# One planner for another on VectorE's side work in an attention and token-mixing block

## The chip, the cores and the metric

One core of a Trainium2 chip runs the whole program. The metric is the device time of one execution in microseconds (us). Each kernel is timed in several executions and the median is given; beside the times there is one execution recorded by the hardware profiler, whose trace has every instruction on TensorE (matrix products; PE in the profile, PEld for its weight loads), VectorE (DVE), ScalarE (ACT), GpSimd (POOL) and SyncE (SP, which issues the DMAs).

## The reference

The block has two halves with residual connections, each modulated by six vectors that come from a condition c. Sizes: S = 2048 rows, D = 512, H = 32 heads of 16, F = 1792.

```python
mod = (silu(c) @ w_mod).reshape(c.shape[0], 6, 1, -1)   # sa, ca, ga, sb, cb, gb
h = layernorm(x) * (1 + ca) + sa
x = x + ga * A(h)          # A: attention over a sliding window of 256 keys, then @ wo
h = layernorm(x) * (1 + cb) + sb
x = x + gb * B(h)          # B: layernorm(h), then an MLP over the rows (tokens):
                           # u = gelu(einsum('bsd,sf->bdf', h, w1) + b1)
                           # y = einsum('bdf,fs->bds', u, w2) + b2, transposed back
```

So every row block passes three layer norms: the first before the projections, the second after attention, and the third, the last, at the start of B.

## The kernel before

The rows are sixteen blocks of 128 (`xres[0..15]`), in four stages `tg` of four blocks. The program has a set-up (to 15.6 us: condition vector, first norm of stage 0, its first Q, K and V), an attention part, and then the MLP.

**Attention, units and sets.** Attention runs as 80 units `(tg, g8, k)`: stage, group of eight heads, and one of five kinds `k`. In texts, units are numbered u = 20 tg + 5 g8 + k, and ul = 5 g8 + k is the place in the stage. Five units with one `(tg, g8)` are called a set. Kinds k = 0, 2 (even heads) and k = 3, 4 (odd heads) compute whole 128-row tiles of scores, and k = 1 the remaining half tiles of both. A unit does, in the program's order:

1. two exponentials on ScalarE (L535), each over a PSUM tile `pss` of 1024 columns (for k = 0 and 3 of stage 0, 512), with other work between them;
2. the scores of the next unit on TensorE (L486 and L513, with masks added by L494 and L522), which read `QT` and `KT` of their set;
3. where k = 1 or 4, the end of a half of the heads: the last products with V (L566) into `po`, and on VectorE the transpose of `po` to `t2` (L592), which frees `po`;
4. a group of dense products (L250) into the one PSUM tile `dn`, for instance Q, K or V for some heads of this stage or the next, the output projection of a finished row block (`wo_group`), or TensorE transposes of normed rows (L232); and an instruction that empties `dn` ("the emptying"), mostly on VectorE: `QT` L291, `ks` L294, `VaugT` L270, `x` L347, `h1T` L240, `part` L676;
5. the products of the previous unit's exponentials with V (L546, L566).

Each engine works in the program's order. `dn` and `po` are single buffers, so the next group waits for the emptying, and the next half of the heads for the transpose. `pss` has three buffers.

**VectorE's side work** is cut into steps which are placed among the units as the program is built:

- quotient: reciprocal of the softmax sums (`zr`, L600), then on GpSimd the product with them (`merge`, L601); then `back`, the transpose back into `OTd` (L608), which `wo_group` reads in the next stage;
- first norm: statistics (`ln1_stats`, L211, L212), on GpSimd a power for 1/sigma (L198, L202), the application (`xn1`, L218), read by TensorE's transposes of the next stage;
- second and third norm (`ln23`, for row blocks 0 to 11): statistics of `x` (p1), application into `h2` (L623) with two products on GpSimd (L634, L635) (p2), statistics of `h2` (p3), application into `hb` (L623) (p4). `hb` is read by four early groups of the MLP (`part_group`, units 72 to 79) and by the MLP.

In the kernel before, each step has a cost in us and a gap in units to the next step of its chain. `run_dve` (L650) is called once per unit, behind the second exponential and ahead of the emptying, with a budget of what `now` is ahead of `load`; `now` grows by 1.5 or 1.9 per unit, and `load` by the costs that were placed. It takes steps chain after chain while they fit.

**Groups** are laid at fixed places of each stage in `plan` (L683). K of stage 0's first two head groups is masked into even and odd heads on VectorE, all others on GpSimd (`KT`, L297).

**Loads.** SP issues all DMAs in the program's order. `at_unit` (L723) puts four w_mod loads at units 1 to 4, `wod` at unit 6, and from unit 22 on one row block of w1 (448 KB) per unit into `w1a`, which takes the place of the released `wmod`. The rest of w1 and w2 are loaded behind the attention part.

**The MLP** (L828, L915, L935) follows, with the last four row blocks' output projection and norms (L847 to L891) among the first.

Of the kernel before, what the change touches and what calls it, by code (L numbers as in the profile page):

```python
# [12 lines left out]
P = 128  # L13
# [11 lines left out]
NA = 11  # L25


@with_exitstack
def kernel(
# [28 lines left out]
    small = ctx.enter_context(tc.tile_pool(name="small", bufs=4))  # L58
# [111 lines left out]
    npool = tc.alloc_tile_pool(name="npool", bufs=2)  # L170
    NG = NT // 4
# [44 lines left out]
    def ln1_apply(tg, tl):  # L216
        xn1[tg, tl] = xp.tile([P, D], DT.bfloat16, name="xn1")
        nc.vector.tensor_scalar(  # L218
            out=xn1[tg, tl][:], in0=xres[4 * tg + tl][:], scalar1=ln1[tg][:, tl, 0:1],
            scalar2=ln1[tg, tl // 2][:, tl % 2 : tl % 2 + 1], op0=ALU.subtract, op1=ALU.mult,  # L220
        )
# [147 lines left out]
    with tc.manual_schedule():  # L369
# [223 lines left out]

        def norm_rest(tg, g8):
# [3 lines left out]
            def quotient():  # L598
# [5 lines left out]
                )  # L604

# [3 lines left out]
            return [(quotient, 0.4, 1), (back, 0.7, 0)]  # L609


        def ln23(tb):
# [9 lines left out]
            def apply(out, src, key):  # L622
                nc.vector.tensor_scalar(  # L623
# [4 lines left out]
            def p1():  # L628
                stats(xres[tb][:], "m2")

            def p2():
                v["h2"] = npool.tile([P, D], DT.bfloat16, name="h2")
                apply(v["h2"][:], xres[tb][:], "m2")
                nc.gpsimd.tensor_tensor(out=v["h2"][:], in0=v["h2"][:], in1=bc_cb1[:], op=ALU.mult)  # L634
                nc.gpsimd.tensor_tensor(out=v["h2"][:], in0=v["h2"][:], in1=bc_sb[:], op=ALU.add)  # L635

            def p3():
                stats(v["h2"][:], "m3")

            def p4():  # L640
                done.add(tb)
                apply(hb[tb][:], v["h2"][:], "m3")
            return [(p1, 0.9, 2), (p2, 0.45, 2), (p3, 0.9, 2), (p4, 0.45, 0)]

        dve = []

        def add_dve(u, ps):
            dve.append([list(ps), u])

        def run_dve(u, budget):  # L650
            spent = 0.0
            for chain in dve:
                while chain[0] and chain[1] <= u and spent + chain[0][0][1] <= budget:
                    f, cost, gap = chain[0].pop(0)
                    f()
                    spent += cost
                    chain[1] = u + gap
            dve[:] = [c for c in dve if c[0]]
            return spent
# [20 lines left out]
        BC = ((4, bc_cb1, True), (2, bc_ga, False), (5, bc_gb, False), (3, bc_sb, False))  # L680
        wo_next = iter(range(12))

        def plan(tg):  # L683
# [6 lines left out]
            for n in range(2, 4):  # L690
                lay(n - 2, v_group(tg, n, ps_dn, act=tg == 0))
            own = ((2, 1, "q"), (3, 1, "k"), (4, 2, "k"), (5, 2, "q"), (6, 3, "k"), (7, 3, "q")) if tg == 0 else (
                (3, 1, "q"), (4, 2, "k"), (5, 2, "q"), (6, 3, "k"), (8, 3, "q"))
            for ul, g8, kind in own:
                lay(ul, qk_group(tg, g8, kind, ps_dn))
            if tg == 0:
                lay(8, bias_group(ps_dn))
                for ul, (v, dst, add1) in zip((9, 17, 18, 19), BC):
                    lay(ul, bc_group(v, dst, add1, ps_dn))
                then[17] = [(lambda g=g: fold_wod(g), 0.45, 0) for g in range(ND)]  # L700
            for ul in {0: (), 1: (7, 9, 10, 14), 2: (7, 9, 10, 14), 3: (7, 9, 10, 11)}[tg]:
                tb = next(wo_next)
                lay(ul, wo_group(tb, ps_dn))
                then[ul] = ln23(tb)
            if tg + 1 < NG:
                t0, t1, k0, v0, q0, k1, v1 = (10, 11, 12, 13, 14, 15, 16) if tg == 0 else (11, 12, 13, 15, 16, 17, 18)
# [4 lines left out]
                for ul, g8, kind in ((k0, 0, "k"), (q0, 0, "q"), (k1, 1, "k")):  # L711
                    lay(ul, qk_group(tg + 1, g8, kind, ps_dn))
# [267 lines left out]
```

## Time and profile before

| | us |
|---|---|
| median of 3 timed runs (lowest to highest) | 294.87 (294.27 to 297.1) |
| the profiled execution, its own time | 295.69 |
| its span, first to last instruction | 294.0 |
| busy: TensorE / VectorE / ScalarE / GpSimd | 256.3 / 170.5 / 170.2 / 99.2 |
| first exponential starts, last ends | 15.59, 193.51 |
| in 18.00 to 195.70: TensorE / VectorE / ScalarE / GpSimd busy | 148.09 / 123.88 / 146.59 / 84.52 |
| MLP: first product, last output product | 195.71, 290.0 |

The span is that of one recorded execution; its own time is 1.7 us longer than its span. Busy times say little by themselves: in the attention part no engine is busy all the time, and what sets the length is read from what each engine waits for. A row of the profile names line, engine, operation and tiles; "idle before ... <-" is the time in which the engine had nothing to run, and the instruction that ended that wait. "issue" there means that the engine waited for nothing that the profile shows. TensorE's granted clock was 0.99 on the mean; from 4.77 us on it was 1.0, but for 0.5 from 32.08 to 35.49 us.

### The profile page before, as it was taken

How to read it: one execution, taken by the hardware profiler on the slowest of the kernel's cores; microseconds unless marked ns; L12 is line 12 of the kernel's file. 1: busy time of each engine (PE TensorE's matmuls, PEld its weight loads, DVE VectorE, ACT ScalarE, POOL GpSimd, SP SyncE). 2: the span in 40 equal slices, each digit the busy share in tenths (PEclk: the TensorE clock that was granted, in tenths of full speed). 3: DMA queues.
4: the chain of work that ended last, by engine and by line, in shares of the span. 5: the costliest groups of instructions: out<-in, count | busy, mean ns of one | idle time of the engine just before them, and what ended most of it. 6: DMA issues, size and time to landing. Idle time of an engine off the chain costs nothing.

```text
span 294.0 us, 12957 instructions
## 1 busy us (share of the span) xinstructions
PE 256.3 (87%) x5960; PEld 140.6 (48%) x5960; DVE 170.5 (58%) x358; ACT 170.2 (58%) x192; POOL 99.2 (34%) x163
## 2 busy tenths in 40 slices
PE   6867798995696987888986998989999999999994
PEld 2534355553454654555654655644444444444441
DVE  6465477665387778687777667888911100505253
ACT  7567677897587899789898898933008220000000
POOL 5020343311134784375486656594410000000000
PEclk9999799999999999999999999999999999999999
DMA  6958000059200000000000000089950000112031
GB/s 195 345 174 291 4 4 6 4 193 401 102 6 2 4 4 4 6 3 4 4 4 4 4 4 4 4 274 401 419 224 1 2 0 0 36 39 71 0 107 36
DMA packets 15386, 24.95 MB, mean 85 GB/s; under 512 B 2276, under 2 KB 11492, under 8 KB 15332
## 3 DMA queue, kind: packets, MB, share of 16 engines
q1 hardware_dynamic: 15332, 24.13, 22.9%
q8 instruction: 46, 0.75, 1.1%
q14 instruction: 8, 0.07, 0.1%
HBM read 22.03 MB, written 2.10 MB: 82 GB/s over the span
## 4 chain that ended last, share of the span: by engine, by line
PE 68%; DVE 16%; POOL 5%; issue 4%; DMA 2%; ACT 2%; SPq 1%; DVEq 0%
PE dn L250 17%; PE py L935 16%; PE pu L828 7%; PE pu L915 7%; PE pss L513 4%; PE po L566 4%; PE pss L486 4%; DVE t L592 4%; PE po L546 3%; POOL merge L601 3%; DMA wmod<-in_w_mod_dram 2%; ACT et L535 2%; DVE zr L600 2%; DVE ks L294 2%; PE pss L494 1%
## 5 line engine op out<-in xcount | busy, mean ns | idle before, releaser
L535 ACT ACTIVATE et<-pss 128x1024 bf16<-128x1024 f32 (+1 forms) x160 | 146.7, 980 | 28.8 <-PE pss L494 20.0
L935 PE MATMUL py<-guT,w2r 128*128 128x512 bf16 x224 | 48.5, 380 | 0.0
L942 DVE SCALAR_TENSOR_TENSOR o<-py,bFM,bc_gb 128x512 bf16<-128x512 f32 x16 | 11.4, 747 | 45.1 <-PE py L935 45.1
L250 PE MATMUL dn<-h1T,wqkv 128*32 128x512 bf16 x512 | 34.3, 390 | 3.6 <-DVE h1T L240 1.5
L486 PE MATMUL pss<-QT,KT 32*128 32x192 bf16 (+2 forms) x704 | 26.3, 240 | 10.1 <-DVE QT L291 3.7
L935 PEld LDWEIGHTS <-w2r 128*128 128x128 bf16 x224 | 21.9, 98 | 26.4
L601 POOL TENSOR_TENSOR merge<-t,zr 128x512 bf16<-128x512 f32 x16 | 17.0, 1060 | 40.7 <-DVE zr L600 40.7
L592 DVE STREAM_TRANSPOSE t<-po 128x512 f32<-128x512 f32 x32 | 22.9, 716 | 12.8 <-PE po L566 12.2
L546 PE MATMUL po<-et,VaugT 128*32 128x192 bf16 (+2 forms) x704 | 25.6, 242 | 3.7 <-DVE t L592 2.1
L546 PEld LDWEIGHTS <-VaugT 128*32 128x32 bf16 x704 | 17.2, 97 | 17.7 <-issue 5.8
L202 POOL TENSOR_TENSOR ln_rstd<-ln_ve,mhalf 128x1 f32<-128x1 f32 (+1 forms) x40 | 24.0, 599 | 3.3
L198 POOL TENSOR_SCALAR ln_ve<-ln_mv 128x1 f32<-128x1 f32 (+1 forms) x40 | 9.7, 243 | 43.3 <-DVE ln_mv L212 20.5
L486 PEld LDWEIGHTS <-KT 32*128 32x128 bf16 x704 | 11.7, 93 | 20.7 <-issue 14.6
L566 PE MATMUL po<-et,VaugT 64*32 64x64 bf16 x960 | 19.2, 193 | 2.0 <-DVE VaugT L270 1.4
L494 PE MATMUL pss<-mask_q,mask_k 32*128 32x64 bf16 (+1 forms) x736 | 18.7, 197 | 1.8 <-issue 1.8
L291 DVE CAST QT<-dn 128x512 bf16<-128x512 f32 x15 | 10.3, 687 | 15.0 <-PE dn L250 11.0
L250 PEld LDWEIGHTS <-wqkv 128*32 128x32 bf16 x512 | 11.8, 97 | 13.9 <-issue 3.8
L250 PE MATMUL dn<-wqkv,h1T 128*32 128x512 bf16 x256 | 16.6, 381 | 0.7 <-DVE ks L294 0.5
L297 POOL TENSOR_SCALAR KT<-ks,mask_even 128x512 bf16<-128x512 bf16 x14 | 9.7, 691 | 21.8 <-DVE ks L294 21.8
L494 PEld LDWEIGHTS <-mask_k 32*128 32x128 bf16 x736 | 15.7, 94 | 2.3 <-issue 2.1
L566 PEld LDWEIGHTS <-VaugT 64*32 64x32 bf16 x960 | 11.1, 92 | 11.4 <-issue 5.6
L513 PE MATMUL pss<-QT,KT 32*64 32x64 bf16 x1024 | 14.6, 195 | 1.6 <-issue 1.5
(112 smaller groups left out, 358.2 us busy)
## 6 DMA issues: line engine op xcount, KB each, us to landing
w2r<-in_B_w_dram SPq DMA_DIRECT2D x14, 512.0 KB, 9.9
w1a<-in_B_w_dram SPq DMA_DIRECT2D x11, 448.0 KB, 8.2
wmod<-in_w_mod_dram SPq DMA_DIRECT2D x6, 512.0 KB, 5.7
w1b<-in_B_w_dram SPq DMA_DIRECT2D x5, 448.0 KB, 6.1
x<-in_A_x_dram SPq DMA_DIRECT2D x16, 128.0 KB, 3.3
out_dram<-otile SPq DMA_DIRECT2D x16, 128.0 KB, 1.7
wqkv<-in_A_wqkv_dram SPq DMA_DIRECT2D x2, 384.0 KB, 5.7
wqkv<-in_A_wqkv_dram SPq DMA_DIRECT2D x1, 512.0 KB, 6.5
```

What stands on the lines that cost most here:

```text
L202: nc.gpsimd.tensor_tensor(out=r[:], in0=ve[:], in1=mhalf[:, 0:n], op=ALU.pow)
L250: nc.tensor.matmul(out[cols, :], lhsT=lhsT[:, cols], rhs=rhs, start=start, stop=stop, tile_position=(0, 32 * j), skip_group_check=True,)
L486: nc.tensor.matmul(pss[j // 2][:, j % 2, c0 : c0 + nq], lhsT=keys(kb, g8, par)[rows[j], k0 : k0 + P], rhs=QT[tg][g8][rows[j], q0 : q0 + nq ...
L494: nc.tensor.matmul(pss[j // 2][:, j % 2, c0 : c0 + 64 * nb].rearrange("p (b q) -> p b q", q=64), lhsT=mask_k[rows[j], P * what : P * what ...
L513: nc.tensor.matmul(pss[a][64 * half : 64 * half + 64, j % 2, c0 : c0 + 64], lhsT=keys(kb, g8, par)[rows[j], k0 : k0 + 64], rhs=QT[tg][g8][ ...
L535: act = nc.scalar.activation(out=et[:, :, 0:n], in_=state.pop((u, a))[:, :, 0:n], func=ACT.Exp, scale=SCORE_SCALE,)
L546: nc.tensor.matmul(state["po"][32 * j : 32 * j + 32, q0 : q0 + nq], lhsT=VaugT[kb // 4][:, kb % 4, 8 * g8 + 2 * j + par, :], rhs=state["e" ...
L566: mm = nc.tensor.matmul(state["po"][32 * j : 32 * j + 32, q0 : q0 + 64], lhsT=VaugT[kb // 4][part64, kb % 4, 8 * g8 + 2 * j + par, :], rhs ...
L592: nc.vector.transpose(out=state["t2"][:, par, :], in_=state["po"][:])
L601: nc.gpsimd.tensor_tensor(out=m[:].rearrange("p (b a d) -> p a b d", a=2, d=DH), in0=t2v[:, :, :, 0:DH], in1=zr[:].to_broadcast([P, 2, 16, ...
L828: nc.tensor.matmul(pu[:, i, :], lhsT=w1_of(sc, fc), rhs=hb[sc][:], start=(sc == 0), stop=(sc == NT - 1),)
L935: nc.tensor.matmul(pys[tl][:], lhsT=w2r[:, fc, tb * P : (tb + 1) * P], rhs=guT[fc][:], start=(fc == 0), stop=(fc == NF - 1),)
```

## The change

The lists of VectorE's steps are now placed with a running estimate of each engine's time (`clock`), kept as the program is built: TensorE, ScalarE, VectorE, GpSimd, and the times at which `dn` and `po` come free. `fill(until)` places steps whose estimated start and end lie ahead of `until`; a step whose predecessor's GpSimd work has not come back by the estimate waits. It is called before `po` is transposed, before each emptying, and at the end of a unit.

The first norm's application goes from VectorE to GpSimd for stages 1 to 3, and that of the third norm (`hb`) for row blocks 0 to 11, now issued together with its statistics. `h2` has a pool of four buffers of its own, and at most four blocks are between p2 and p3. Statistics of stages 2 and 3 are computed in stage 0. Q, K, V, `wo` and `bc` groups are laid at other units; the unit without a group changes from ul 2 and 19 (stage 1, 2), 2 (stage 3) to ul 16 and 19 (stage 1, 2), 11 (stage 3). Each w1 row block is loaded in two halves of 224 KB by 22 DMAs. The number of matmuls is the same.

```diff
-    small = ctx.enter_context(tc.tile_pool(name="small", bufs=4))
+    small = ctx.enter_context(tc.tile_pool(name="small", bufs=6))
...
+    lnpool = tc.alloc_tile_pool(name="lnpool", bufs=LIVE)
...
     def ln1_apply(tg, tl):
         xn1[tg, tl] = xp.tile([P, D], DT.bfloat16, name="xn1")
-        nc.vector.tensor_scalar(
+        (nc.gpsimd if tg else nc.vector).tensor_scalar(
...
-            return [(quotient, 0.4, 1), (back, 0.7, 0)]
+            return [(quotient, 0.36), (back, 0.72)]
...
             def p3():
                 stats(v["h2"][:], "m3")
-
-            def p4():
+                apply(nc.gpsimd, hb[tb][:], v["h2"][:], "m3")
                 done.add(tb)
-                apply(hb[tb][:], v["h2"][:], "m3")
-            return [(p1, 0.9, 2), (p2, 0.45, 2), (p3, 0.9, 2), (p4, 0.45, 0)]
+                live.discard(tb)
+                return 1.54
+            return [(p1, 0.88), (p2, 0.37, lambda: len(live) < LIVE), (p3, 0.88)]
...
-        def run_dve(u, budget):
-            spent = 0.0
-            for chain in dve:
-                while chain[0] and chain[1] <= u and spent + chain[0][0][1] <= budget:
...
+        def on_pool(cost):
+            clock["pool"] = max(clock["pool"], clock["dve"]) + cost
+            return clock["pool"] + 0.1
+
+        def fill(until):
+
+            while True:
+                for chain in chains:
+                    f, cost, *free = chain[0][0]
+                    start = max(clock["dve"], chain[1])
+                    if start + cost <= until and start < clock["dve"] + 0.3 and all(x() for x in free):
+                        break
+                else:
+                    break
+                chain[0].pop(0)
+                clock["dve"] = start + cost
+                given = f()
+                chain[1] = on_pool(given) if given else clock["dve"]
+                chains[:] = [c for c in chains if c[0]]
...
             if tg == 0:
+                for ul, g8, kind in ((2, 1, "k"), (3, 1, "q"), (4, 2, "k"), (5, 2, "q"), (6, 3, "k"), (7, 3, "q")):
+                    qk(ul, tg, g8, kind)
                 lay(8, bias_group(ps_dn))
-                for ul, (v, dst, add1) in zip((9, 17, 18, 19), BC):
+                for ul, (v, dst, add1) in zip((9, 16, 17, 18), BC):
...
+            else:
+                for ul, g8, kind in ((2, 1, "q"), (3, 2, "k"), (4, 2, "q"), (5, 3, "k"), (8, 3, "q")):
+                    qk(ul, tg, g8, kind)
+                for ul in (6, 7, 9, 10):
...
-                t0, t1, k0, v0, q0, k1, v1 = (10, 11, 12, 13, 14, 15, 16) if tg == 0 else (11, 12, 13, 15, 16, 17, 18)
+                t0, t1, k0, v0, q0, k1, v1 = (10, 11, 12, 13, 14, 15, 19) if tg == 0 else (11, 12, 13, 14, 15, 17, 18)
...
-                w1box["sc"] = iter(range(NA))
-
-            sc = next(w1box.get("sc", iter(())), None)
-            if sc is not None:
-                dma.dma_start(out=w1box["a"][:, sc, :], in_=w1box["v"][:, sc, :])
+                w1box["sc"] = iter([(sc, n) for sc in range(NA) for n in range(2)])
+
+            for sc, n in [x for x in [next(w1box.get("sc", iter(())), None)] if x]:
+                part_f = slice(n * F // 2, (n + 1) * F // 2)
+                dma.dma_start(out=w1box["a"][:, sc, part_f], in_=w1box["v"][:, sc, part_f])
...
             if closes:
+                clock["pe"] += 0.23
+                fill(clock["pe"])
                 close_head_set(*closes, behind)
-                load += 0.75
+                clock["dve"] = max(clock["dve"], clock["pe"] + 0.05) + 0.73
...
             emit_exp(u, 1)
-            load = max(load, now - 0.5)
-            now += 1.5 if (tg, k) in ((0, 0), (0, 3)) else 1.9
-            load += run_dve(u, min(now - load, 1.3 if group and group[2] else 1.9))
+            clock["act"] = max(clock["act"], ready[u][1]) + half
             if group:
-                group[1](tile_)
-                load += group[2]
+                fill(clock["pe"] + 0.05)
+                evacuate(group, tile_, tg == 0 and ul < 2)
...
+            fill(clock["pe"])
             at_unit(tg, ul, u)
```

## The prediction

> **What bounds the kernel now.** I read the busy times by stretches of 25 us first, then the start of every exponential on ScalarE (two per unit, so 80 unit lengths), then the waits inside the attention stage, then the order of time around its longest gaps. From 195.7 us on TensorE never pauses, as in this stretch (columns: length, then busy us of PE, PEld, DVE, ACT, POOL, then clock and DMA):
>
> ```profile
> 225.00:250.00 25.00, 25.00 (x118) 11.33 (x116) 1.99 (x4) 5.54 (x9) 0.00 (x0) 1.00 0.00 1
> ```
>
> So the last 98 us are TensorE's, and the change leaves their matmuls alone. The attention stage (15.6 to 193.5) is where time is lost. A set of five units repeats sixteen times; four sets, by the same view:
>
> ```profile
> 84.93:96.67 11.74, 9.27 (x360) 6.13 (x345) 8.84 (x18) 9.70 (x12) 4.18 (x8) 1.00 0.02 4
> 150.76:162.49 11.73, 8.07 (x344) 5.29 (x329) 8.64 (x17) 9.67 (x12) 8.18 (x12) 1.00 0.02 4
> 162.49:172.77 10.28, 9.79 (x376) 6.09 (x362) 7.93 (x15) 9.57 (x11) 6.08 (x12) 1.00 0.02 5
> 183.54:193.51 9.97, 9.10 (x336) 5.49 (x336) 8.16 (x18) 9.56 (x11) 6.69 (x10) 1.00 0.13 42
> ```
>
> ScalarE works 9.6 us in every set and TensorE 8.1 to 9.8; the sets last 9.97 to 11.7. The floor is 9.97: ScalarE is then idle 0.4 us. The twelve sets from 59.64 to 193.51 take 133.87 us, 14.2 over twelve floors. What TensorE waits for there (total us, times, longest):
>
> ```profile
> PE pss L486 <- DVE QT L291: 3.7, 3, 1.6
> PE po L546 <- DVE t L592: 2.1, 3, 1.0
> PE dn L250 <- DVE ks L294: 2.1, 4, 0.9
> PE dn L232 <- DVE h1T L240: 1.8, 2, 1.2
> PE dn L250 <- DVE x L347: 1.6, 2, 0.9
> PE po L566 <- DVE VaugT L270: 1.4, 2, 1.2
> PE pss L494 <- issue: 1.8, 2, 1.4
> ```
>
> VectorE is not full (7 to 9 us a set): its few urgent steps, which empty PSUM, stand behind others. The order of time shows one case, a long norm pair ahead of V, then a wait for GpSimd ahead of Q, each with TensorE's stall:
>
> ```profile
> 156.59 1.38 DVE L623 TENSOR_SCALAR h<-x,ln_mv,ln_rstd 128x512 bf16<-128x512 bf16 x2
> 157.89 0.68 DVE L270 CAST VaugT<-dn 128x512 bf16<-128x512 f32 x1
> ...
> 160.25 0.69 DVE L617 BATCH_NORM_STATS2 ln_stats<-h 128x6 f32<-128x512 bf16 x1 [1.06 <-POOL h L635]
> 161.07 0.66 DVE L291 CAST QT<-dn 128x512 bf16<-128x512 f32 x1
> ```
>
> ```profile
> 158.62 0.21 PE L566 MATMUL po<-et,VaugT 64*32 64x64 bf16 x4 [1.23 <-DVE VaugT L270]
> 161.88 0.40 PE L486 MATMUL pss<-QT,KT 32*128 32x256 bf16 x12 [1.40 <-DVE QT L291]
> ```
>
> A second cause: three stalls that no engine ended, at 67.06 (1.44 us), 73.14 (1.47) and 77.97 (1.79), 4.70 together. The trace's packets of the instruction queue, 16 KB each, begin at 64.72, 70.78 and 75.59: TensorE resumes 2.34 to 2.38 us after each. They fall in or just behind the eleven w1 loads (62 to 75.5 us, about 380 GB/s: 5.05 MB in 13.3 us):
>
> ```profile
> 67.06 0.20 PE L494 MATMUL pss<-mask_q,mask_k 32*128 32x64 bf16 x2 [1.44 <-issue]
> 73.14 0.40 PE L546 MATMUL po<-et,VaugT 128*32 128x256 bf16 x10 [1.47 <-issue]
> 77.97 0.39 PE L486 MATMUL pss<-QT,KT 32*128 32x64 bf16 x10 [1.79 <-issue]
> ```
>
> So 14.2 us over the floor are 4.7 of code loading and 9.5 of late VectorE.
>
> **The change, part by part.** The sum is against the profiled execution, span 294.0, time 295.69, which is 0.82 above the median of the three runs; I apply the difference to the median.
>
> *VectorE's order.* In the built program of the changed kernel, from unit 21 on, a unit mostly issues on VectorE one step that empties PSUM for a group and one other: with k = 1 the transpose of po, k = 2 the reciprocal (L600), k = 3 the transpose back (L608), k = 4 the transpose of po; statistics, now often two together, stand in k = 0, the longest unit (2.24 us), and only in unit 79 does a norm step stand ahead of the transpose of po in its unit. Two steps of 0.69 to 0.72 us, with 0.35 for the reciprocal, are below the 1.82 to 2.19 us of such a unit. In k = 0 two statistics at 0.85 (0.67 + 0.18) and an emptying at 0.69 make 2.39 against 2.24, but the transpose that normally follows comes after the next group's matmuls, so I cost it at nothing; its cover gone, it is 0.15 us each in some ten units. Where does the stall go? ScalarE is next. I take 10.2 us a set, between the best set (9.97) and the best set that follows a late one (10.28), instead of (133.87 - 4.70) / 12 = 10.76: 12 x 0.56 = -6.8. Bounds: 10.45, the mean of sets 130.06 to 150.76 and 162.49 to 183.54, gives -3.8; the floor gives -9.5.
>
> *Moved to GpSimd.* Twelve first norms (L218; the first four blocks stay) and twelve last norms (hb, L623) leave VectorE. Beside GpSimd's work the moved kind is slow: xn1 applies in the stage take 0.40 us with GpSimd idle and 0.67 with it busy, the longest 1.31. So VectorE loses 12 x 0.47 to 0.56 plus 12 x 0.42, about 11 of 124 us; that is part of the term above. GpSimd gains 24 instructions. No first norm is on GpSimd in the trace; the nearest row is the K masking, same shape and kind:
>
> ```profile
> L297 POOL TENSOR_SCALAR KT<-ks,mask_even 128x512 bf16<-128x512 bf16 x14 | 9.7, 691 | 21.8 <-DVE ks L294 21.8
> ```
>
> I take 0.69, with 1.16 (L634) as the upper bound: 16.6 to 27.8 us more on 84.5 of 178. GpSimd's queue is then busy 61 to 67% of a stage of 167 us, and these results are due 3 to 10 units later, so I cost them at nothing, +4 if a late answer reaches TensorE in a third of the sets (1.03 us each, the row L546 waiting for L592).
>
> *Groups re-laid.* QT1 of stages 1 to 3 goes from unit 3 to 2, so that its emptying no longer ends just before the scores that read it (the 1.40 us above, 0.67 at 69.81 and 1.63 at 118.09); that is in the 9.5. Five units stay without a group, but three of them now are k = 1 (36, 56, 71). There TensorE is busy the whole 2.19 us; less sixteen matmuls in 1.0 us, ScalarE's 1.94 us sets the length: 3 x 0.25 = -0.75 (0 to -0.75). Stage 0's own K and Q swap places at units 2 and 3; both are read at unit 4 and the later one ends near 27.3 as before: 0.
>
> *Stage 0.* Seven statistics go into units 1 and 2, where VectorE sat idle 3.96 us before 24.07: 17.8 + 7 x 0.8 = 23.4, ahead of K's emptying at 24.0, so 0. Statistics and reciprocal no longer stand ahead of the emptyings at 36.01, 38.5 and 46.1: 0.16 + 0.5 + 0.35 = -1.0. The half clock from 32.08 to 35.49 (granted 0.5), which follows the code stall that ends at 30.97 behind the w_mod loads, stays: those loads are unmoved. Bounds 0 and -2.7 (1.7 us of clock regained).
>
> *w1 in halves.* Bytes stay, issues go from 11 to 22 at 0.43 us, 9.5 us of SP's queue against 13.2 of transfer, and nothing else stands in that queue before 191 us. The loads are not tied to units: SP issued all eleven in 7.5 us, waiting only for the wmod reader (which moves one unit forward) and for the load eight before. So half as many bytes are in flight, not fewer per microsecond. Counted from TensorE's resumption before it, a code packet begins 1.48 us later with the queues quiet (77.97 to 79.45), 3.72 among the loads (67.06 to 70.78) and 2.45 as they end (73.14 to 75.59). A load puts 28 KB on each of 16 engines; a half puts 14, midway, so I estimate half of the excess: 1.1, 1.1 and 0.5 less, -2.7; a shorter set reaches each chunk's end sooner, +0.5: -2.2. Bounds: 0 (the w_mod loads, in pieces of 1 KB rather than 3.5, left the same 1.47 us stall at 30.97) and -4.7. The Trainium skill ("DMA: Bandwidth & Descriptors", Queues, rings and completion order) says that an engine changes between queues only behind a whole packet of descriptors, typically 9 to 17. By that rule a half makes a packet of eight rows half as long, and the sum keeps at least the 2.2; no run here shows packets. Against the halves the same page (Why a DMA increments its semaphore by 16) wants 2 KiB per partition to fill the queues, and a half has 1.75; that lengthens a transfer that nobody waits for before unit 72.
>
> *The end.* Blocks 10 and 11 finish later: behind the last transposes VectorE waits for GpSimd's two products of block 11, so statistics of block 12 start about 204.2 on the old time line, not 200.22. Four blocks at 3.4 us then end near 218.5; the matmuls that read block 15 start at 219.6 (204.09 + 12 x 1.295). Cost 0, 1 us if the margin is gone.
>
> Sum: -6.8 - 0.75 - 1.0 - 2.2 = -10.75; span 283.3, profiled time 284.9, median **284.1**.
>
> **The rivals.** (a) Only the peaks go: sets fall to 10.45, code stalls stay, 294.87 - 3.8 - 0.5 = 290.6. For it: most sets from 130 us on already are 10.3 to 10.8 with ScalarE idle 0.7 to 1.2 us; against: the waits above, 12.7 us in six kinds, have a VectorE instruction each in front that the new order takes away. 0.18. (b) All goes: -9.5 - 0.75 - 4.7 - 1.0 = 278.9, with the clock dip 277.2. 0.14. (c) No change. GpSimd holds up what VectorE keeps: twelve h applies took 0.32 us at best and 1.15 at worst beside GpSimd; if each now loses 0.83 in front of an emptying, 284.1 + 10 = 294.1. Against: the applies now follow a reciprocal or start before GpSimd's product, where they took 0.32 (189.03). 0.08. The Trainium skill ("SBUF — State Buffer", SBUF: two separate sides) has the two engines share a port pair under a lock for a whole instruction; the 1.31 us beside a product of 1.06 agrees, and by that rule every added GpSimd instruction is a possible block. (d) Slower: GpSimd answers late. In units 35, 55 and 72 four products (4.6 us) and a power (0.84) precede the merge (1.06), and the transpose back, in order on VectorE, would hold an emptying and the next po transpose. It decides once the merge ends more than three units after its reciprocal in most sets: one stall of 1.03 to 1.40 per set is +12.4 to +16.8, so 296.5 to 300.9. For it, 16.6 more us on one in-order queue; against, the transpose back stands four units behind in those places and the merge finds GpSimd free in the others. 0.08, of which 0.06 beyond 1%. (e) The halves do nothing, since the loads still run as one stream: 2.2 comes back, 286.3, within the forecast's band.
>
> **How the numbers follow.** Forecast 0.52, 281 to 287.5. Range 279 to 291: it takes in (a) and the upper half of (b), and leaves out 0.2. I call within 1% (292 to 297.8) no change, about what such a measurement can tell. Faster: 0.52 + 0.18 + 0.14 = 0.84; (c) and a share of (d) make 0.10; slower 0.06.
>
> **What would show it.** Right: sets of 10.0 to 10.3 us from unit 20 on, TensorE's waits for QT, t, ks, x and VaugT below 4 us together, the xn and hb rows on POOL at 0.69, stalls by "issue" near 70 us of some 0.4 to 0.9. Wrong: "issue" stalls of 1.4 again (then +2.2), waits of OTd for merge or of statistics for POOL's h with an emptying behind them, or TensorE waiting for hb near 216 to 220.

## The result and the profile after

| | median, us (lowest to highest) | ratio to the kernel before, 95% interval |
|---|---|---|
| before, beside the changed kernel | 295.46 (294.27 to 297.1) | |
| changed | 311.42 (310.95 to 314.49) | 1.0558, 1.0471 to 1.0646 |

The change makes the kernel 5.6% slower; 284.1 us, 3.7% faster, was forecast. The profiled execution took 311.14 us, its span is 309.4 against 294.0. Ratios leave out executions well above the fastest of their kernel (five of the ten where the halves are tried alone, below); medians and ranges take all.

The page of the changed kernel (line numbers have moved: the dense products are L252, `QT` L293, `t` L594, `merge` L606, `OTd` L614, `h` and `hb` L628, `xn` L220, `KT` L299), its busy times and the clock in 40 slices:

```profile
PE 265.9 (86%) x5950; PEld 144.4 (47%) x5960; DVE 163.1 (53%) x334; ACT 168.9 (55%) x192; POOL 148.2 (48%) x187
PEclk9999799999999995889998799999999999999998
PE 54%; POOL 23%; DVE 11%; issue 5%; ACT 2%; DMA 2%; SPq 1%; POOLq 0%; DVEq 0%
```

VectorE lost 7.4 us of work, in the direction meant (170.5 to 163.1, some 11 were forecast), but GpSimd gained 49.0 (99.2 to 148.2), where the prediction had 16.6 to 27.8. The third line is the share of the engines in the chain that ended last: GpSimd had 5% before and has 23%. The groups on GpSimd tell why:

```profile
L628 POOL TENSOR_SCALAR hb<-h,ln_mv,ln_rstd 128x512 bf16<-128x512 bf16 x12 | 25.1, 2088 | 1.2
L220 POOL TENSOR_SCALAR xn<-x,ln_mv,ln_rstd 128x512 bf16<-128x512 bf16 x12 | 24.9, 2077 | 0.0
L299 POOL TENSOR_SCALAR KT<-ks,mask_even 128x512 bf16<-128x512 bf16 x14 | 9.7, 690 | 19.8 <-DVE ks L296 19.8
```

Each of the 24 moved applications takes 2.08 us. The K masking, the row from which they were priced at 0.69, is unchanged. What the engines waited for (total us, times, longest):

```profile
PE dn L252 <- DVE QT L293: 13.7, 4, 4.7
DVE OTd L614 <- POOL merge L606: 10.9, 6, 5.3
DVE h L628 <- POOL ln_rstd L204: 8.7, 3, 3.2
...
PE po L548 <- DVE t L594: 4.7, 7, 0.8
...
PE pu L880 <- DVE hb L917: 2.9, 2, 1.8
```

Of before's waits for `QT`, `t`, `ks`, `h1T`, `x` and `VaugT`, 12.7 us in sixteen waits, short ones remain (for `t` 4.7 us, each under 0.9). In place of the long ones stand four stalls of 2.4 to 4.7 us, 13.7 together. The chain behind the longest, first GpSimd's order of time:

```profile
124.91 2.07 POOL L220 TENSOR_SCALAR xn<-x,ln_mv,ln_rstd 128x512 bf16<-128x512 bf16 x1
...
127.94 2.08 POOL L628 TENSOR_SCALAR hb<-h,ln_mv,ln_rstd 128x512 bf16<-128x512 bf16 x1
...
130.98 2.08 POOL L628 TENSOR_SCALAR hb<-h,ln_mv,ln_rstd 128x512 bf16<-128x512 bf16 x1
133.04 0.69 POOL L299 TENSOR_SCALAR KT<-ks,mask_even 128x512 bf16<-128x512 bf16 x1
133.71 0.69 POOL L299 TENSOR_SCALAR KT<-ks,mask_odd 128x512 bf16<-128x512 bf16 x1
134.36 1.05 POOL L606 TENSOR_TENSOR merge<-t,zr 128x512 bf16<-128x512 f32 x1
```

then VectorE's:

```profile
128.18 0.34 DVE L605 RECIPROCAL zr<-t 128x32 f32<-128x32 f32 x1
129.41 0.69 DVE L349 TENSOR_TENSOR x<-dn,x 128x512 bf16<-128x512 f32 x1 [0.89 <-PE dn L252]
135.45 0.71 DVE L614 STREAM_TRANSPOSE OTd<-merge 128x512 bf16<-128x512 bf16 x1 [5.34 <-POOL merge L606]
136.08 0.65 DVE L293 CAST QT<-dn 128x512 bf16<-128x512 f32 x1
```

and TensorE's:

```profile
131.80 0.30 PE L568 MATMUL po<-et,VaugT 64*32 64x64 bf16 x16
136.79 1.64 PE L252 MATMUL dn<-wod,OTd 128*32 128x512 bf16 x16 [4.69 <-DVE QT L293]
```

The reciprocal ends at 128.52. Its product `merge` could run then, but GpSimd, without a pause since 103.65 (no line of it in that stretch has an idle time), is at the first of two `hb`, with a power between them and a masking behind, and ends `merge` at 135.41. VectorE's next instruction is the transpose back, which needs `merge`; behind it, in order, stands the emptying of Q, whose products had ended at 131.2. So VectorE waits 5.34 us and TensorE 4.69. The stall of 2.42 us at 186.05 is of this kind. The other two, 3.21 at 115.55 and 3.37 at 169.34, have the third line of the waits in front: an `h`, placed ahead of the emptying of Q, waits for the power (L204), which stands on GpSimd behind an `hb` and two products.

The stalls cost more than their length. Three lengths of a set, starting at 117.73, 131.97 and 148.07 (columns: length, then busy us of PE, PEld, DVE, ACT, POOL, then clock, DMA share, GB/s):

```profile
117.73:131.97 14.24, 13.46 (x376) 7.47 (x368) 6.60 (x13) 9.49 (x10) 13.78 (x13) 0.68 0.02 4
131.97:148.07 16.10, 10.86 (x364) 7.00 (x354) 8.99 (x17) 9.43 (x11) 6.14 (x10) 0.89 0.01 4
148.07:157.93 9.86, 8.95 (x348) 5.69 (x345) 7.50 (x15) 9.46 (x11) 8.55 (x12) 1.00 0.01 3
```

The first of them holds no stall of over 0.7 us, yet it takes 14.24: from 116.62 to 126.86, behind the stall that ended at 115.55, TensorE was granted half its clock (0.68 in the mean), and its work grew to 13.46 us. The third is below the 9.97 that the prediction called the floor. Over the attention part the half clock was granted for 23.9 us, 20.5 of them in and behind these stalls; before it was 3.4.

Stalls by code loading are still there; TensorE's order of time at the w1 loads:

```profile
66.55 0.20 PE L496 MATMUL pss<-mask_q,mask_k 32*128 32x64 bf16 x2 [1.27 <-issue]
71.65 1.04 PE L252 MATMUL dn<-h1T,wqkv 128*32 128x512 bf16 x14 [0.86 <-issue]
77.29 0.39 PE L252 MATMUL dn<-h1T,wqkv 128*32 128x512 bf16 x2 [2.10 <-issue]
```

They sum to 4.23 us against 4.70. Where the 15.4 us of span went, by the starts of the exponentials: first exponential 0.3 earlier, sets 0 to 3 unchanged (44.0 us), the twelve others 147.4 against 133.9 (+13.5), what follows the last exponential 102.8 against 100.5 (+2.3).

### The profile page after: what moved, and what is told of

Same layout as the page of the kernel before. It is cut to its first block, busy times and chain, and to the rows that moved or that the text cites. A ratio compares the mean times of both kernels' runs of the same rounds, so it can differ in the third digit from the quotient of the medians.

```text
span 309.4 us, 12967 instructions
## 1 busy us (share of the span) xinstructions
PE 265.9 (86%) x5950; PEld 144.4 (47%) x5960; DVE 163.1 (53%) x334; ACT 168.9 (55%) x192; POOL 148.2 (48%) x187
## 4 chain that ended last, share of the span: by engine, by line
PE 54%; POOL 23%; DVE 11%; issue 5%; ACT 2%; DMA 2%; SPq 1%; POOLq 0%; DVEq 0%
PE dn L252 17%; PE py L987 16%; POOL hb L628 7%; PE pu L967 7%; PE pss L488 3%; POOL h L641 3%; PE po L548 3%; POOL ln_rstd L204 3%; POOL xn L220 3%; POOL h L642 3%; PE pss L515 3%; PE po L568 2%; POOL KT L299 2%; POOL merge L606 2%; DMA wmod<-in_w_mod_dram 2%
## 5 line engine op out<-in xcount | busy, mean ns | idle before, releaser
L537 ACT ACTIVATE et<-pss 128x1024 bf16<-128x1024 f32 (+1 forms) x160 | 145.4, 985 | 43.4 <-PE pss L496 23.9
L252 PE MATMUL dn<-h1T,wqkv 128*32 128x512 bf16 x512 | 38.3, 420 | 11.9 <-DVE QT L293 6.6
L987 PEld LDWEIGHTS <-w2r 128*128 128x128 bf16 x224 | 21.9, 98 | 26.4
L488 PE MATMUL pss<-QT,KT 32*128 32x192 bf16 (+2 forms) x704 | 27.7, 244 | 4.6 <-ACT et L537 3.5
L548 PE MATMUL po<-et,VaugT 128*32 128x192 bf16 (+2 forms) x704 | 26.8, 250 | 4.8 <-DVE t L594 4.7
L594 DVE STREAM_TRANSPOSE t<-po 128x512 f32<-128x512 f32 x32 | 22.9, 715 | 9.0 <-PE po L568 8.4
L548 PEld LDWEIGHTS <-VaugT 128*32 128x32 bf16 x704 | 18.4, 101 | 18.8 <-issue 8.3
L606 POOL TENSOR_TENSOR merge<-t,zr 128x512 bf16<-128x512 f32 x16 | 16.9, 1057 | 21.0 <-DVE zr L605 21.0
L628 POOL TENSOR_SCALAR hb<-h,ln_mv,ln_rstd 128x512 bf16<-128x512 bf16 x12 | 25.1, 2088 | 1.2
L204 POOL TENSOR_TENSOR ln_rstd<-ln_ve,mhalf 128x1 f32<-128x1 f32 (+1 forms) x40 | 23.8, 596 | 3.2
L220 POOL TENSOR_SCALAR xn<-x,ln_mv,ln_rstd 128x512 bf16<-128x512 bf16 x12 | 24.9, 2077 | 0.0
L252 PEld LDWEIGHTS <-wqkv 128*32 128x32 bf16 x512 | 13.0, 100 | 24.8 <-issue 16.4
L252 PE MATMUL dn<-wod,OTd 128*32 128x512 bf16 x192 | 13.5, 403 | 7.4 <-DVE QT L293 7.1
L296 DVE CAST ks<-dn 128x512 bf16<-128x512 f32 x16 | 11.0, 689 | 16.1 <-PE dn L252 15.3
L299 POOL TENSOR_SCALAR KT<-ks,mask_even 128x512 bf16<-128x512 bf16 x14 | 9.7, 690 | 19.8 <-DVE ks L296 19.8
```

The costliest lines, as they stand in the source:

```text
L204: nc.gpsimd.tensor_tensor(out=r[:], in0=ve[:], in1=mhalf[:, 0:n], op=ALU.pow)
L220: (nc.gpsimd if tg else nc.vector).tensor_scalar(out=xn1[tg, tl][:], in0=xres[4 * tg + tl][:], scalar1=ln1[tg][:, tl, 0:1], scalar2=ln1[tg ...
L252: nc.tensor.matmul(out[cols, :], lhsT=lhsT[:, cols], rhs=rhs, start=start, stop=stop, tile_position=(0, 32 * j), skip_group_check=True,)
L488: nc.tensor.matmul(pss[j // 2][:, j % 2, c0 : c0 + nq], lhsT=keys(kb, g8, par)[rows[j], k0 : k0 + P], rhs=QT[tg][g8][rows[j], q0 : q0 + nq ...
L537: act = nc.scalar.activation(out=et[:, :, 0:n], in_=state.pop((u, a))[:, :, 0:n], func=ACT.Exp, scale=SCORE_SCALE,)
L548: nc.tensor.matmul(state["po"][32 * j : 32 * j + 32, q0 : q0 + nq], lhsT=VaugT[kb // 4][:, kb % 4, 8 * g8 + 2 * j + par, :], rhs=state["e" ...
```

## The experiments

Each run has a short name, given in brackets behind its time.

**Is it the applications or the new order?** Both applications go back to VectorE; order, groups and w1 halves stay. As the plan has it, a first norm's application is then charged with nothing on VectorE.

```diff
-        (nc.gpsimd if tg else nc.vector).tensor_scalar(
+        nc.vector.tensor_scalar(
...
                 stats(v["h2"][:], "m3")
-                apply(nc.gpsimd, hb[tb][:], v["h2"][:], "m3")
+                return 0.85
+
+            def p4():
+                apply(nc.vector, hb[tb][:], v["h2"][:], "m3")
                 done.add(tb)
                 live.discard(tb)
-                return 1.54
-            return [(p1, 0.88), (p2, 0.37, lambda: len(live) < LIVE), (p3, 0.88)]
+            return [(p1, 0.88), (p2, 0.37, lambda: len(live) < LIVE), (p3, 0.88), (p4, 0.3)]
```

> The changed kernel with both applications (first norm of stages 1 to 3, third norm of blocks 0 to 11) back on VectorE; planner, groups and w1 halves stay. Theory P (a first- or third-norm application takes 2.08 us on GpSimd, not the 0.69 that the planner and I took, so GpSimd answers late and the whole loss is this): no wait of OTd for merge or of h for ln_rstd above 1 us, TensorE's waits for QT on L252 near 0, granted clock at 1.0 after 36 us, sets from unit 20 on at 9.8 to 10.4 us, time 282 to 289 us. Rival O (the new order or the re-laid groups lose by themselves): 298 us or more, with the long waits near units 44, 50, 64 and 70 still there. Between, 289 to 298, both have a part.

287.35 us (e1), ratio 0.9725 (0.9676 to 0.9775). The changed kernel becomes 2.8% faster than the one before by this edit alone. The same kernel again, for its trace:

> The same kernel as e1_norms_vector, again, since the profiled execution of the first ran at half clock throughout: the profile is wanted, and the time beside the two that follow. 285 to 289 us; sets from unit 20 on 9.8 to 10.5 us except where code stalls fall (units 23 to 27); no stall of TensorE above 1 us ended by VectorE.

287.96 us (e1b), ratio 0.9712 (0.9636 to 0.9788), span 289.0. Its waits:

```profile
PE po L548 <- DVE t L594: 5.5, 8, 0.8
DVE ln_stats L622 <- POOL h L642: 2.5, 1, 2.5
...
DVE OTd L614 <- POOL merge L606: 0.6, 2, 0.4
...
PE dn L252 <- DVE QT L293: 0.2, 1, 0.2
```

TensorE's wait for `QT` went from 13.7 to 0.2 and VectorE's for `merge` from 10.9 to 0.6. So the whole loss hangs on where the 24 applications run, and what is left of the change (order, groups and halves together) is a gain. Not all of the expectation came: outside units 20 to 29 four sets last 10.8 to 12.7 us, and the longest, the last, has a stall of 1.22 us by "issue" at 179.58 and 3.4 us at half clock behind it.

**Why 2.08 us?** Behind the MLP's groups in the kernel before, with GpSimd idle, six forms of the instruction were added, each twice, on a 128x512 bf16 tile. They do work beyond the reference's.

```diff
...
+        for n, (a, b, o0, o1) in enumerate((
+            (s1, s2, ALU.subtract, ALU.mult), (s1, s2, ALU.mult, ALU.add),
+            (s1, 1.0, ALU.subtract, ALU.mult), (s1, 0.0, ALU.mult, ALU.add),
+            (1.0, s2, ALU.subtract, ALU.mult), (1.0, 1.0, ALU.subtract, ALU.mult),
+        )):
+            for r in range(2):
+                dst = gtmp.tile([P, D], DT.bfloat16, name=f"form{n}")
+                g.tensor_scalar(out=dst[:], in0=src[:], scalar1=a, scalar2=b, op0=o0, op1=o1)
```

> The kernel before, plus twelve instructions on GpSimd while it is idle in the MLP, six forms of the two-step scalar instruction on 128x512 bf16, twice each, results unused: (1) subtract column, multiply column, (2) multiply column, add column, (3) subtract column, multiply constant, (4) multiply column, add constant, (5) subtract constant, multiply column, (6) subtract and multiply constants. Theory 2P (the second column operand is what costs): 2.08 us for 1 and 2, 0.69 for 3 to 6. Rival S (the subtraction costs): 2.08 for 1, 3, 5, 6 and 0.69 for 2 and 4. Time as before, within 1%.

297.61 us (e3, one execution). GpSimd's order of time; the first line is one of the form with two constants, then the forms follow in the order written:

```profile
216.50 1.94 POOL L935 TENSOR_SCALAR form<-hb 128x512 bf16<-128x512 bf16 x1
218.44 2.08 POOL L935 TENSOR_SCALAR form<-hb,cols 128x512 bf16<-128x512 bf16 x1
...
222.57 1.52 POOL L935 TENSOR_SCALAR form<-hb,cols 128x512 bf16<-128x512 bf16 x2
224.07 1.99 POOL L935 TENSOR_SCALAR form<-hb,cols 128x512 bf16<-128x512 bf16 x1
...
228.69 0.69 POOL L935 TENSOR_SCALAR form<-hb,cols 128x512 bf16<-128x512 bf16 x1
229.37 2.00 POOL L935 TENSOR_SCALAR form<-hb,cols 128x512 bf16<-128x512 bf16 x1
```

Every form that subtracts takes 1.92 to 2.08 us, with columns or constants; product and sum take 0.77 with two columns (1.52 for the pair) and 0.69 with one. A second column adds less than 0.1, so the theory that the second column is the cost falls. What goes with the 2 us is a subtraction ahead of a product. A sum ahead of a product was not run, so it is not shown whether the subtraction itself is slow or the order of the two steps. For an elementwise operation with one tensor input the Trainium skill ("GPSIMD Engine Reference", 4.1 Engine selection) expects roughly line rate of GpSimd. What line rate is, no run here shows; but the forms with a subtraction take 2.7 times as long as product and sum on the same tile, so the one rule does not hold for both.

**The cheap form in the changed kernel.** x * rstd + (-mean * rstd), in place of (x - mean) * rstd, both applications on GpSimd:

```diff
+    def mul_add(out, src, mean, rstd):
+        shift = small.tile([P, 1], DT.float32, name="shift")
+        nc.gpsimd.tensor_scalar(
+            out=shift[:], in0=mean, scalar1=rstd, scalar2=-1.0, op0=ALU.mult, op1=ALU.mult,
+        )
+        nc.gpsimd.tensor_scalar(
+            out=out, in0=src, scalar1=rstd, scalar2=shift[:], op0=ALU.mult, op1=ALU.add,
+        )
...
```

> The changed kernel with its 24 applications still on GpSimd, but as x * rstd + (-mean * rstd), multiply and add with two columns, which took 0.77 us in e3, behind one small instruction for the shift; planner, order and halves as in the change. Theory S (only the subtract form is slow, and the loss is its price): rows of 0.77 us, no wait of VectorE for GpSimd above 1.2 us, time 282 to 288 us, near e1b. Rival C (twenty-four more tile instructions on GpSimd lose by themselves, by its queue or by what they hold up on VectorE): 292 us or more.

296.75 us (e8), ratio 1.0016 (0.9974 to 1.0057): 14.7 us of the loss are gone, and no gain is there yet, so the time falls to rival C (292 or more). The applications on GpSimd:

```profile
L223 POOL TENSOR_SCALAR xn<-x,ln_rstd,shift 128x512 bf16<-128x512 bf16 x12 | 9.2, 763 | 1.3
L223 POOL TENSOR_SCALAR hb<-h,ln_rstd,shift 128x512 bf16<-128x512 bf16 x12 | 9.1, 762 | 1.2
```

With the shift (0.27) one is 1.03, still above the 0.69 that the plan assumes, and one late `merge` is left: VectorE's order of time, with TensorE's wait of 3.72 us for the `QT` behind it at 128.09:

```profile
126.75 0.71 DVE L627 STREAM_TRANSPOSE OTd<-merge 128x512 bf16<-128x512 bf16 x1 [4.38 <-POOL merge L619]
127.39 0.65 DVE L306 CAST QT<-dn 128x512 bf16<-128x512 f32 x1
```

**Is it GpSimd's load or the plan's wrong price?** First the changed kernel with its slow form, the plan told 2.08 where it had 0.69 (and 2.93 for 1.54, a last norm with its power):

```diff
-                return 1.54
+                return 2.93
...
-                    return 0.69
+                    return 2.08
```

> The changed kernel, with the planner told 2.08 us for each application on GpSimd (0.69 to 2.08, 1.54 to 2.93); all else as in the change. If only the plan was wrong: VectorE's steps are placed behind GpSimd's answers, its waits above 2 us vanish, time 284 to 291 us. If GpSimd is simply too full (24 x 1.4 us more, about 134 of 165 us): late answers stay, time 296 to 311 us.

295.5 us (e2), ratio 0.9977 (0.9928 to 1.0025). The same instructions of the same length, placed by their real price, save 15.9 us. The time lies between the two theories' ranges. VectorE's wait for `merge` fell from 10.9 to 5.2 us, the longest 1.8; its waits of over 2 us for GpSimd are gone from the attention part, and two (4.69 and 2.87) stand behind it. TensorE's largest stall is now for a first norm that comes late:

```profile
131.41 0.45 PE L234 MATMUL dn<-identity,xn 128*128 128x128 bf16 x5 [2.55 <-POOL xn L220]
```

I put that stall down to the load: GpSimd had no idle time from 116 to 134 us. That another order of its work in that stretch would have avoided it is not ruled out. Then both, the cheap form and its price (1.05 for 0.69, 1.9 for 1.54 in the kernel with `mul_add`):

> The kernel of e8_mul_add (both applications on GpSimd as product and sum, measured 0.76 us and 0.27 us for the shift), and the planner is told that price: 1.05 us for a first norm in place of 0.69, 1.9 for a last norm with its power in place of 1.54. Theory 'mispriced': e8 is still 9 us above the kernel with both applications on VectorE only because the planner thinks GpSimd some 0.35 us per application faster than it is, so that a step behind GpSimd is placed too early in a few places; told the price, the late merge of the set that took 15.21 us goes (no wait of OTd for merge over 2 us), no set is over 13.5 us behind the first, and the time comes to 287 to 291 us. Rival 'capacity': GpSimd as it is loaded (about 104 us in the attention part) answers too late wherever it is placed; the time stays at 293 us or more, with the steps behind GpSimd moved later and waits of OTd for merge, or TensorE for xn, again at 2 us or more. The earlier pair of this kind (the price told, subtract form) gave 295.5 us, with one stall of 2.55 us where TensorE waited for xn.

290.98 us (e9), ratio 0.9855 (0.9789 to 0.9921), its interval clear of the untold one. One wait of 2.17 us for `merge` is left and one stall of 1.52 for `QT`. That is inside the 287 to 291 of "mispriced", at its upper end, and the wait of over 2 us that was to be gone is there. The time is 3.0 to 3.6 us above the two runs with both applications on VectorE (287.96 and 287.35), so the load, rightly priced, still seems to have a small part.

**Which application?** One of the two on GpSimd in the slow form, the other on VectorE. First norms on GpSimd:

> The changed kernel with the third norm's application on VectorE and the first norm's on GpSimd in the subtract form: 12 of the 24 slow instructions, eight of them from unit 20 on, bunched in units 21 to 25 and 41 to 45. If the loss goes by where the slow ones bunch: a long stall near units 42 to 45 only, 289 to 296 us; if it goes by their number: half of the loss, 298 to 301 us.

292.78 us (e6, one execution), within the 289 to 296 of the first theory; there is one long stall, 3.51 us, in unit 49 (42 to 45 were named). Last norms on GpSimd:

> The changed kernel with the first norm's application back on VectorE and the last norm's (hb) on GpSimd in the subtract form (12 x 2.08 us); the other half of the pair with e6_xn_gpsimd (292.78 us, its longest stall 3.51 us). If the cost of the changed kernel goes with the microseconds that the two kinds of application put on GpSimd, half the load gives about what e6 gave, 291 to 297 us, with one or two long waits of OTd for merge. If hb, issued together with its power in one step and ahead of merge, is the worse half, it gives 300 us or more with three or more such waits; if it is harmless, 288 to 290 us.

305.39 us (e7, one execution), with four stalls of 2.5 to 3.4 us:

```profile
PE dn L252 <- DVE QT L293: 11.7, 4, 3.4
...
DVE h L628 <- POOL ln_rstd L204: 7.5, 3, 3.1
DVE OTd L614 <- POOL merge L606: 7.3, 4, 3.5
```

Equal microseconds on GpSimd, 12.6 us apart, on one execution each: the last norm is the worse half. Two of its four stalls are a late `merge`. The two others are an `h` that waits for its power behind `hb`, as in the changed kernel.

**The halves.** The kernel before with w1 in halves and nothing else:

```diff
-                w1box["sc"] = iter(range(NA))
+                w1box["sc"] = iter([(sc, n) for sc in range(NA) for n in range(2)])
...
```

> The kernel before with nothing changed but w1 loaded in halves. If a half load halves what a code packet waits (my forecast): the three code stalls near 67, 73 and 78 us, 4.70 us before, come to 2.0 to 2.5, time 2 us less (ratio 0.993). If the stream of loads is what counts, not the size of one (as the trace of the changed kernel suggests, with 1.27, 0.86 and 2.10): stalls of 4 to 5 us together, time within 0.4% of before.

295.1 us (e4), ratio 0.9915 (0.987 to 0.996): 2.5 us less by the ratio (1.2 to 3.8), 0.7 by the medians (295.81 before, beside it), so a gain is likely and its size open. In the two traces, the two sets at the loads (units 20 to 29) take 21.9 us in place of 25.3. TensorE's waits by "issue", of before's 4.7 at the loads:

```profile
PE pss L494 <- issue: 0.7, 1, 0.7
PE po L566 <- issue: 0.2, 1, 0.2
PE pu L828 <- issue: 0.2, 1, 0.2
```

None of them lies at the loads: all three stalls there are gone, more than either theory had. And the kernel of e1b with w1 in whole row blocks:

> e1b_norms_vector with w1 loaded in eleven whole row blocks, as before the change. If halves help (as alone in the kernel before, where no code stall was left and 2.5 us were gained): code stalls of 4 to 5 us near 65 to 78 us and 1.5 to 3 us slower than e1b. If they don't once the attention part is dense (as in the changed kernel's trace, 4.2 us of stalls with halves): the same time within 0.8 us.

289.19 us (e5), ratio 0.976 (0.9693 to 0.9827), 1.2 us above e1b, within both intervals. Its stalls at the loads (1.67, 1.09 and 0.18) are not longer than e1b's three (1.48, 0.86, 1.28). In the new order the halves are not shown to gain anything, and the new order gains without them.

**A version to keep.** Only the first norms on GpSimd, as product and sum, the plan told 1.05:

> A version that may beat both kernels: both norms as in e1b_norms_vector, but the twelve first norms are applied on GpSimd as product and sum (0.27 + 0.76 us), the planner told 1.05 us for each; the last norm stays on VectorE. GpSimd gets 12.4 us more than in e1b (82.0 us in the attention part), VectorE loses 12 x 0.4 to 0.67 = 5 to 8 us. Theory 'GpSimd's lateness is what costs, and 1 us pieces are short enough': 286 to 289 us, at or 1 us below e1b (287.96), with no stall behind merge or xn over 1 us. Rival 'VectorE was no longer the bound in e1b, so nothing is gained, and any GpSimd work ahead of merge costs': 290 us or more, with a wait of OTd for merge or of TensorE for xn that e1b has not.

288.48 us (e10), ratio 0.9763 (0.9691 to 0.9835), in the first theory's range, though one wait for `merge` is 1.13. Its attention part is the shortest so far, 168.0 us from first to last exponential against 177.9 before, but it starts 1.5 us later, and behind it TensorE waits 2.6 us for `hb`. So the two products of `h` for row blocks 10 and 11 went to VectorE, where the MLP's own take 0.42 against GpSimd's 1.15, and the plan is told so:

```diff
+                engine = nc.vector if tail else nc.gpsimd
+                engine.tensor_tensor(out=h2[:], in0=h2[:], in1=bc_cb1[:], op=ALU.mult)
+                engine.tensor_tensor(out=h2[:], in0=h2[:], in1=bc_sb[:], op=ALU.add)
...
```

> The version of e10_xn_mul_add, with the two products of h for row blocks 10 and 11 on VectorE. In e10 the end behind the attention part loses 2.6 us where TensorE waits for hb of the last blocks (1.57 and 1.03): VectorE stood 1.68 and 1.12 us for GpSimd's products of blocks 10 and 11 (1.15 each), which take 0.42 to 0.43 each on VectorE in the MLP's own norms. Theory 'the end has no margin and these two waits use it up': both waits go, TensorE's waits for hb fall below 0.5 us, the time comes to 285.5 to 287.5 us, ratio 0.966 to 0.972 against e10's 0.976. Rival 'the end is set elsewhere (by the power and the four blocks' own steps, 3.0 us a block)': the waits for hb stay at 1.5 us or more and the time at 288 to 289 us.

288.31 us (e12), ratio 0.9744 (0.9697 to 0.9792). TensorE's waits for `hb`, one line each, e10's first and then the edited kernel's:

```profile
PE pu L895 <- DVE hb L932: 2.6, 2, 1.6
```

```profile
PE pu L898 <- DVE hb L935: 1.0, 1, 1.0
```

The waits for GpSimd's product went and 1.6 us of the stall with them, though not below 0.5; the median moved by 0.2. The time is the rival's (288 to 289), the waits are neither theory's, and a gain is not shown. The kernel with both applications on VectorE (287.35 and 287.96) and the two versions with the cheap first norms on GpSimd (288.48, 288.31) beat both kernels and cannot be told apart; the plainest is the first, with the norms where they were.

## Why the prediction was wrong

**The step that failed** is "Moved to GpSimd": "the nearest row is the K masking, same shape and kind ... I take 0.69, with 1.16 (L634) as the upper bound", and behind it "I cost them at nothing". The masking multiplies and adds a constant, the application subtracts and multiplies; on GpSimd that is 0.69 against 2.08, and the bound of 1.16 was no bound. The row shared shape, types and opcode, and the operation inside was taken for granted. With 2.08 the moved load is 49.9 us, not 16.6 to 27.8; GpSimd is busy for 125.4 us of the attention part (some of its work now falls behind it), where the prediction had 101 to 112. The second half of the step fails by itself too: with the cheap form, rightly priced, GpSimd is busy there for 103.0 us, within what was predicted, and that kernel (e9) is still 3.0 to 3.6 us slower than with both applications on VectorE; that is near the 4 that the prediction named and left out.

**The price stood in the plan as well.** The kernel's own code says 0.69 for this application, and I took the same number from a row without asking whether the row had a subtraction in it. With a wrong price in the plan a late answer is not an accident of the three places that rival (d) named: the transpose back is placed where the estimate says the product is ready. Told the price, the kernel came from 311.42 to 295.5 us; with a cheap form, from 311.42 to 296.75; with both, to 290.98; with both applications back on VectorE, to 287.35 and 287.96.

**Rival (d)** was right that GpSimd answers late with an emptying behind the waiting instruction, at a chance of 0.08. Its mechanism, the transpose back behind a late `merge`, stands in front of two of the four stalls; in front of the other two is `h`, waiting for its power, a wait that no part of the prediction had. It put one stall of 1.03 to 1.40 us into every set. There are four, 13.7 us, and the five sets with them and behind them take 70.7 us, 20.8 over five of 9.97. Of the 7.1 us beyond the stalls, 6.9 lie in three sets with the half clock (the fourth stall, without one, added its own length alone). (d) did not price that, though the prediction had such a dip behind a code stall before its eyes. Its places (units 35, 55, 72) were wrong too: the stalls came in units 44, 50, 64 and 70, behind one to three pieces of 2.08 us among GpSimd's other work.

**Rival (c)**, GpSimd slowing what VectorE keeps, is not what decided: `h` on VectorE takes 0.406 us in the median and 1.154 at worst, against 0.392 and 1.146 before.

**VectorE's order, -6.8,** holds in part where GpSimd does not spoil it. The ten sets behind the loads, six to fifteen, last 10.86 us in the mean before; 10.2 was taken. With both applications on VectorE they last 10.41 (e5) and 10.64 (e1b, with the disturbed last set); 10.25 and 10.23 are reached in e10 and e12, where the first norms are on GpSimd as product and sum. Undisturbed sets of 9.86 are below the floor of 9.97, which was only the best set seen. In the changed kernel itself the gain was buried: 12.27.

**Stage 0, -1.0,** did not come in this pair: sets 0 to 3 take 44.0 us in both traces. It does show where the traces are alike: with 3.4 us of half clock between 20 and 25 us in each, these sets take 42.87 us in the old order (e3) and 41.65 and 41.82 in the new one (e1b, e10). What took it in the changed kernel is not settled; its stall by code at 31.03 was 1.80 us against 1.47 before. **Groups re-laid, -0.75,** cannot be told from the order; no run separates them.

**The halves, -2.2,** may have the right size in the old order (2.5 by the ratio, 0.7 by the medians) but not in the new one, where 4.23 of 4.70 us of stalls stay: a term read from one order was added to a change that moves the code's stalls.

**The end, 0 or 1 if the margin is gone:** 2.85 us of TensorE's waits for `hb`, and 2.3 more behind the last exponential. The 218.5 and 219.6 of the prediction left 1.1 us for a chain that GpSimd then held up by 2.36, 2.50 and 2.85 (the three waits on VectorE between 214 and 223).

Against the sum, the span of 283.3 was missed by 26 us: 23.3 in the twelve sets (19.7 in the five named, against 10.2 each, 1.7 in code stalls that stayed, 1.9 in the other seven), 1.0 in sets 0 to 3, 2.3 at the end, and 0.3 the other way ahead of the first exponential.

## What to carry to other kernels

A step that changes engines is priced by a row with the same operations in it, not only the same opcode and shape; where the trace has none, the price is open on the upper side, and one measured form of it is worth more than the rest of the sum. A plan with due times is only as good as its prices: an error of 1.4 us per step on an in-order queue became stalls of 2.4 to 4.7 us where one to three of them stand ahead of an urgent one. Before moving work off a busy engine ask who waits, in order, for the answer: there the unloaded engine stands still.

## What the hardware showed that was not expected

- GpSimd's scalar instruction with a subtraction ahead of a product takes 1.92 to 2.08 us on 128x512 bf16, with product and sum 0.69 to 0.77; the application takes 0.31 us at best on VectorE and 0.38 to 0.41 in the median (e1b).
- Behind a stall of TensorE its granted clock may halve: 3.21 us of stall were followed by 10.2 us at 0.5, 4.69 by 3.4, 3.37 had 6.8 (from its middle on), and one of 2.42 none. The Trainium skill ("TensorE: Matmul & The Clock Gate", Part 1: The HAM clock gate) has the clock halved after some 3.4 us of idle time and restored after as much activity; the stretches at 0.5 are multiples of 3.4, which agrees. But in the stretch of 10.2 us TensorE was busy for 9.7, so as much activity did not restore the clock there; and e12 has a stretch at 0.5, 74.5 to 77.9, behind stalls of only 1.40 and 1.55, so the length of the single stall does not decide it alone.
- Stalls by "issue" beside w1's transfers are there in the traces of the new order, up to 2.1 us a time, whether w1 comes whole or in halves; only the old order with halves has none. The one of 1.22 us at 179.58 in e1b came with no load under way, 2.4 us behind the start of a packet of the instruction queue, about the distance that the prediction found. What decides it stays open.
